# Two paddings in the allocation of SBUF: the start addresses of all matmul operands of an attention and two feed-forward layers

## The chip, the cores and the metric

The kernel runs on one core of a Trainium2 chip. The metric is device time in microseconds (us). The kernel before took 1613.8 us, the median of three runs (1612.5 to 1614.32).

## The reference

Two batches of 3008 tokens go through an attention without softmax and then, as 6016 tokens of 256 features, through two feed-forward layers with 2048 hidden features:

```
scores = (z @ z.T) / S                 # z: 2 x 3008 x 64
x = u * (max(scores, 0)**2 @ v)        # u, v: 2 x 3008 x 256
h = x @ w_in1;  g = where(h > 0, h, exp(min(h, 0)) - 1);  x = g @ w_out1
h = x @ w_in2
g = (a0 + a1 h + a2 h^2 + a3 h^3) / (1 + |b0| |h| + |b1| h^2 + 1e-6)
return g @ w_out2
```

The weights come as 64-bit floats and are brought to single precision on the chip.

## The kernel before, in words

Every product is computed in three matmuls on float32r operands: each float32 matrix is held as a rounded part (hi) and the rest (lo), and hi·hi, lo·hi and hi·lo are summed in PSUM. A matmul has a moving operand (`rhs`, here up to 512 columns, 4 bytes each, so 2048 bytes in each partition) and a stationary one (`lhsT`, 128 columns, 512 bytes), which a weight load brings into the array beforehand. The weight load of the next matmul runs while the present one streams.

The program has two stages. In the attention (about the first 520 us), queries are taken in spans of up to 512 columns (ten of 512 and two of 448), keys in chunks of 128. Here a matmul uses 64 of the 128 rows of the array, and two of them, on the two halves of the rows, run at the same time; the text calls them a pair. For each two chunks the PE does three pairs of scores (line 292) and then twelve pairs of values (line 329). Of one span of 512 columns that is 36 pairs of scores and 141 of values (the last chunk is a half). In the feed-forward part the tokens are taken in tiles of 512 columns (nine) and then 448, 384, 320 and 256. `hidden` (lines 263 to 265 in `mm3`, and 399, 400 and 402) and `project` use all 128 rows, 12 matmuls of a layer and of 128 hidden features. The order of all of this is written out by hand, step by step; VectorE, ScalarE and GpSimd work on other steps of it in the meantime.

Where a tile lies in SBUF follows from the order of the pools and their sizes, in each partition from address 0 on:

- a scratch of 16384 bytes for transfers that GpSimd would describe, reserved by the program object; then 128 bytes with four small constants;
- pool `wp`, 32 buffers of 4096 bytes (tag `w`): the split values V and all split weights. It starts at 16512, so all of its buffers and all of the 512-byte slices used as stationary operands start at 128 modulo 512. At the end of the program some tiles of the last feed-forward tile (256 columns) lie there too;
- pool `cp`, one tile `coef` of 6 floats (a and b of the last layer), which takes 32 bytes, at 147584;
- pool `sp`, everything else (tags `q`, `raw`, `rl`, `hl`, `x`, `x2`, `t`, `r`, `xo`, `e`), from 147616 on, in buffers of 2048 or 4096 bytes, so that all of them start at 160 modulo 512.

So the moving operand of a matmul starts at 160 modulo 512 in all 9240 matmuls but 96: those at the end take `w` tiles at 128. The stationary operand starts at 128 (V and weights), and at 160 in the 864 matmuls of the scores, whose two operands are both Z tiles (`rl`, `x2`, `t`, `r` of pool `sp`). A weight load in line 329 or in a feed-forward line reads at 128, one in line 292 at 160, and what streams beside it is the matmul before it in the program. No operand's start is 0 modulo 512.

## Time and profile before

| | |
|---|---|
| median of the three runs | 1613.8 us |
| span of the profiled execution | 1611.0 us |
| PE busy | 1569.5 us (97%), 9240 matmuls |
| VectorE (DVE) busy | 1392.3 us (86%) |
| ScalarE (ACT) busy | 1326.0 us (82%) |
| GpSimd (POOL) busy | 723.9 us (45%) |

The profile is of one execution, whose span (first to last instruction) is 2.8 us under the median of the runs. Matmuls are pipelined: the profile's duration of one (about 395 ns for 512 columns) is longer than the distance from its start to the next one's start, so busy time of PE says little, and the count of matmuls in a stretch says how fast they follow each other.

### The profile page before, as it was taken

To read this page: it belongs to the slowest core of one execution; us is meant where nothing else is said; L and a number is where in the kernel's file an instruction comes from. 1 tells how busy PE (TensorE), PEld (TensorE's weight loads), DVE (VectorE), ACT (ScalarE), POOL (GpSimd) and SP (SyncE) were. 2 spreads that over 40 slices of the span, in tenths; PEclk is the share of its full clock that TensorE was granted. 3 is DMA by queue.
4 is the path that set the end of the run, shared out by engine and by line. 5 is a ranking of instruction groups with operands and counts; after the bars stand their busy time and mean duration, and the time that the engine had idled before them with its cause. 6 is when DMAs were issued, how large, how long until landed. Compare 5 with 4: busy or idle time off the path is not lost.

```text
span 1611.0 us, 25201 instructions
## 1 busy us (share of the span) xinstructions
PE 1569.5 (97%) x9240; PEld 1321.5 (82%) x9240; DVE 1392.3 (86%) x1915; ACT 1326.0 (82%) x2123; POOL 723.9 (45%) x590
## 2 busy tenths in 40 slices
PE   8999999999999999999999999999999999999986
PEld 6888897898778778787878787887878888999976
DVE  7788889888886478989898988889898999999998
ACT  6777776877776788988888888988888888999886
POOL 3344542443433444445444444444454444444445
PEclk9999999999999999999999999999999999999999
DMA  4243343221222400000000000000000000000000
GB/s 125 66 125 119 112 144 109 66 68 50 75 61 89 157 26 1 27 1 1 27 1 27 1 27 1 27 0 1 25 1 23 1 22 1 20 1 12 11 1 15
DMA packets 38716, 67.16 MB, mean 42 GB/s; under 512 B 4928, under 2 KB 15680, under 8 KB 38592
## 3 DMA queue, kind: packets, MB, share of 16 engines
q1 hardware_dynamic: 38592, 65.55, 13.1%
q8 instruction: 72, 1.18, 0.3%
q14 instruction: 52, 0.43, 0.1%
HBM read 45.88 MB, written 19.66 MB: 41 GB/s over the span
## 4 chain that ended last, share of the span: by engine, by line
PE 66%; DVE 11%; issue 3%; ACT 3%; POOL 1%; POOLq 0%; ACTq 0%; DVEq 0%
PE psum L329 11%; PE psum L264 9%; PE psum L399 9%; PE psum L402 9%; PE psum L265 9%; PE psum L400 9%; PE psum L263 9%; PE psum L292 3%; DVE x L526 2%; DVE t L528 1%; DVE q L503 1%; DVE q L527 1%; DVE e L432 1%; DVE t L509 1%; ACT t L480 1%
## 5 line engine op out<-in xcount | busy, mean ns | idle before, releaser
L533 POOL TENSOR_TENSOR x<-t,r 128x512 fp32r<-128x512 f32 (+3 forms) x190 | 233.9, 1231 | 509.4 <-DVE t L528 443.3
L329 PE MATMUL psum<-hl,w 64*128 64x512 f32 (+1 forms) x2256 | 395.2, 391 | 3.7 <-ACT xo L349 2.6
L329 PEld LDWEIGHTS psum<-hl,w 64*128 64x128 f32 x2256 | 279.7, 185 | 44.4 <-ACT xo L349 6.4
L329 PE MATMUL psum<-x,w 64*128 64x512 f32 (+1 forms) x1128 | 293.1, 388 | 1.0 <-DVE x L305 1.0
L441 POOL TENSOR_TENSOR hl<-e,hl 128x512 fp32r<-128x512 f32 (+3 forms) x200 | 246.8, 1234 | 35.4 <-ACT hl L440 29.6
L295 ACT ACTIVATE w<-psum 128x1024 f32<-128x1024 f32 (+1 forms) x144 | 145.5, 1011 | 111.3 <-PE psum L292 109.8
L298 DVE SCALAR_TENSOR_TENSOR psum<-psum,w 128x1024 f32<-128x1024 f32 (+1 forms) x144 | 173.8, 1207 | 57.9 <-ACT w L295 57.2
L480 ACT ACTIVATE t<-psum,coef 128x512 f32<-128x512 f32 (+3 forms) x200 | 150.6, 753 | 78.8 <-PE psum L402 77.4
L503 DVE SCALAR_TENSOR_TENSOR q<-q,coef,psum 128x512 f32<-128x512 f32 (+3 forms) x190 | 135.3, 712 | 72.1 <-ACT q L496 71.5
L305 DVE TENSOR_TENSOR x<-psum,hl 128x1024 fp32r<-128x1024 f32 (+1 forms) x144 | 172.9, 1201 | 12.0 <-ACT q L200 0.5
L329 PEld LDWEIGHTS psum<-x,w 64*128 64x128 f32 x1128 | 168.0, 185 | 17.3 <-DVE x L305 1.5
L264 PE MATMUL psum<-hl,w 128*128 128x512 f32 (+4 forms) x416 | 157.2, 378 | 4.8 <-POOL hl L441 4.5
L399 PE MATMUL psum<-x,w 128*128 128x512 f32 (+4 forms) x416 | 155.6, 376 | 2.0 <-ACT x L451 1.4
L264 PE MATMUL psum<-x,w 128*128 128x512 f32 (+3 forms) x384 | 147.8, 385 | 8.5 <-POOL x L533 8.5
L263 PE MATMUL psum<-hl,w 128*128 128x512 f32 (+4 forms) x416 | 155.6, 374 | 0.2 <-ACT hl L440 0.2
L399 PE MATMUL psum<-rl,w 128*128 128x512 f32 (+4 forms) x416 | 155.5, 376 | 0.0
L265 PE MATMUL psum<-hl,w 128*128 128x512 f32 (+4 forms) x416 | 155.3, 373 | 0.0
L400 PE MATMUL psum<-x,w 128*128 128x512 f32 (+4 forms) x416 | 154.7, 374 | 0.0
L400 PE MATMUL psum<-rl,w 128*128 128x512 f32 (+4 forms) x416 | 154.4, 373 | 0.0
L296 ACT ACTIVATE hl<-w 128x1024 fp32r<-128x1024 f32 (+1 forms) x144 | 150.6, 1046 | 4.6
L432 DVE SCALAR_TENSOR_TENSOR e<-e,psum 128x512 f32<-128x512 f32 (+3 forms) x200 | 129.8, 649 | 27.8 <-ACT e L427 21.8
L526 DVE SCALAR_TENSOR_TENSOR x<-t,coef,r 128x512 fp32r<-128x512 f32 (+3 forms) x190 | 150.2, 791 | 0.0
(143 smaller groups left out, 3683.2 us busy)
## 6 DMA issues: line engine op xcount, KB each, us to landing
raw<-w_in_dram SPq DMA_DIRECT2D x16, 512.0 KB, 3.9
raw<-w_out_dram SPq DMA_DIRECT2D x16, 512.0 KB, 3.8
wd<-q SPq DMA_DIRECT2D x28, 256.0 KB, 2.3
raw<-wd SPq DMA_DIRECT2D x14, 512.0 KB, 3.4
raw<-v_dram SPq DMA_DIRECT2D x22, 256.0 KB, 2.9
raw<-uT_dram SPq DMA_DIRECT2D x10, 512.0 KB, 3.8
xd<-xo SPq DMA_DIRECT2D x20, 256.0 KB, 2.2
outT_dram<-xo SPq DMA_DIRECT2D x18, 256.0 KB, 2.2
```

The source lines that it names most:

```text
L263: nc.tensor.matmul(out, lhsT=lh, rhs=rh, start=start, stop=False)
L264: nc.tensor.matmul(out, lhsT=lh, rhs=rl, start=False, stop=False)
L265: nc.tensor.matmul(out, lhsT=ll, rhs=rh, start=False, stop=stop)
L298: nc.vector.scalar_tensor_tensor(out=s, in0=s, scalar=SCALE, in1=e, op0=ALU.mult, op1=ALU.mult)
L305: nc.vector.tensor_tensor(out=lo[:, :, :w], in0=psum[:, i:i + 2, :w], in1=f(hi[:, :, :w]), op=ALU.subtract)
L329: nc.tensor.matmul(acc[ti][d, h][:, :w], lhsT=lhs[rows, j % 2, d * P:(d + 1) * P], rhs=rhs[rows, :w], start=j == 0 and k == 0, stop=k == 2 ...
L399: nc.tensor.matmul(h[:, cols], lhsT=wh[:, d, c], rhs=x[d][0], start=d == 0, stop=False)
L400: nc.tensor.matmul(h[:, cols], lhsT=wl[:, d, c], rhs=x[d][0], start=False, stop=False)
L441: nc.gpsimd.tensor_tensor(out=lo, in0=e, in1=f(hi), op=ALU.subtract)
L480: act(new("p", "t", 3), h, AF.Identity, bias=a2, scale=a3)
L526: stt(out=st["hi"], in0=st["top"], scalar=a0, in1=st["r"], op0=ALU.add, op1=ALU.mult)
L533: eng.tensor_tensor(out=st["lo"], in0=st["p"], in1=st["r"], op=ALU.mult)
```

## The change

The pool `cp` is made first, before `wp`. Its tile `coef` gets 480 floats (1920 bytes), of which the first 6 are used; the others are a filler and are never written or read. The scratch is 8192 bytes instead of 16384. With that `coef` lies at 8320, `wp` starts at 10240 (20 times 512) and `sp` at 141312 (276 times 512). All buffers of both pools then start at 0 modulo 512, and so do both operands of all 9240 matmuls. Every operand of the other engines that lies in these pools moves along. No instruction is added, removed or moved on any engine, no wait changes, and each tile shares its buffer with the same other tiles as before.

```
-    wp = ctx.enter_context(tc.tile_pool(name="wp", bufs=32))
     cp = ctx.enter_context(tc.tile_pool(name="cp", bufs=1))
+    wp = ctx.enter_context(tc.tile_pool(name="wp", bufs=32))
     sp = ctx.enter_context(tc.tile_pool(name="sp", bufs=2))
...
-    coef = cp.tile([P, 6], F32, name="coef")
+    coef = cp.tile([P, 480], F32, name="coef")[:, :6]
...
-    nc = bacc.Bacc("TRN2", target_bir_lowering=False, num_devices=1)
+    nc = bacc.Bacc("TRN2", target_bir_lowering=False, num_devices=1, dynamic_dma_scratch_size=8192)
```

## Rows read from the trace of the kernel before

**Rows 1.** The page: busy time, slices of PE and its clock, chain that ended last
```profile
span 1611.0 us, 25201 instructions
PE 1569.5 (97%) x9240; PEld 1321.5 (82%) x9240; DVE 1392.3 (86%) x1915; ACT 1326.0 (82%) x2123; POOL 723.9 (45%) x590
...
PE   8999999999999999999999999999999999999986
...
PEclk9999999999999999999999999999999999999999
...
PE 66%; DVE 11%; issue 3%; ACT 3%; POOL 1%; POOLq 0%; ACTq 0%; DVEq 0%
```
**Rows 2.** Busy us (x instructions) by stretch; then clock, DMA share, GB/s
```profile
0.00:520.00 520.00, 504.94 (x4262) 432.43 (x4264) 435.99 (x447) 385.70 (x462) 211.01 (x171) 1.00 0.31 94
520.00:600.00 80.00, 76.65 (x321) 60.37 (x322) 42.73 (x68) 62.38 (x109) 36.25 (x28) 0.98 0.28 92
600.00:1250.00 650.00, 649.68 (x2778) 520.60 (x2777) 577.49 (x846) 566.06 (x955) 308.36 (x239) 1.00 0.04 12
1250.00:1500.00 250.00, 248.82 (x1261) 223.88 (x1260) 234.42 (x382) 227.12 (x429) 119.09 (x108) 1.00 0.03 9
1500.00:1611.00 111.00, 89.41 (x623) 84.18 (x623) 101.64 (x175) 84.74 (x170) 49.19 (x46) 0.98 0.03 10
```
**Rows 3.** Chain that ended last, 318 to 358: start us, us, what
```profile
322.60 0.69 PE psum L292 x6
323.28 2.79 PE psum L329 x24
...
346.96 0.69 PE psum L292 x6
```
**Rows 4.** Lines 292 and 329: matmuls, duration ns min/median/max, first and last start
```profile
L292 PE MATMUL psum<-rl,t x48: 385/387/393, 32.9 to 333.3; 64*128 64x512 f32 x48
L292 PE MATMUL psum<-rl,r x48: 385/387/393, 39.8 to 340.3; 64*128 64x512 f32 x48
L329 PE MATMUL psum<-hl,w x2256: 358/392/625, 9.0 to 520.2; 64*128 64x512 f32 x158, 64*128 64x448 f32 x30
...
L329 PE MATMUL psum<-x,w x1128: 357/391/625, 10.8 to 520.4; 64*128 64x512 f32 x158, 64*128 64x448 f32 x30
```
**Rows 5.** Matmul groups by shape: line, tiles, count, busy us, mean ns, idle before
```profile
L329 PE MATMUL psum<-hl,w 64*128 64x512 f32 x1880 | 337.3, 395 | 2.8 <-ACT xo L349 1.7 <-ACT hl L296 0.9
L329 PE MATMUL psum<-x,w 64*128 64x512 f32 x940 | 253.6, 392 | 1.0 <-DVE x L305 1.0
L263 PE MATMUL psum<-hl,w 128*128 128x512 f32 x288 | 114.2, 396 | 0.2 <-ACT hl L440 0.2
L265 PE MATMUL psum<-hl,w 128*128 128x512 f32 x288 | 113.8, 395 | 0.0
L265 PE MATMUL psum<-hl,w 128*128 128x448 f32 x32 | 11.8, 369 | 0.0
L265 PE MATMUL psum<-hl,w 128*128 128x384 f32 x32 | 10.9, 339 | 0.0
L265 PE MATMUL psum<-hl,w 128*128 128x320 f32 x32 | 9.9, 309 | 0.0
L265 PE MATMUL psum<-w 128*128 128x256 f32 x32 | 9.0, 282 | 0.0
L263 PE MATMUL psum<-w 128*128 128x256 f32 x32 | 9.0, 282 | 0.0
L263 PE MATMUL psum<-hl,w 128*128 128x256 f32 x32 | 9.0, 280 | 0.0
L265 PE MATMUL psum<-hl,w 128*128 128x256 f32 x32 | 8.9, 279 | 0.0
```
**Rows 6.** The page: large groups of ACT; DMA queue
```profile
L295 ACT ACTIVATE w<-psum 128x1024 f32<-128x1024 f32 (+1 forms) x144 | 145.5, 1011 | 111.3 <-PE psum L292 109.8
L296 ACT ACTIVATE hl<-w 128x1024 fp32r<-128x1024 f32 (+1 forms) x144 | 150.6, 1046 | 4.6
...
q1 hardware_dynamic: 38592, 65.55, 13.1%
```

## The prediction

> **What bounds the kernel now.** I read the page first. PE is busy in 97% of the span, every slice but the first and the last two shows it at 9, and the chain of work that ended last is PE for 66% [rows 1]. Busy time of matmuls is modelled, so I went on to the table by stretches for their number. From 600 to 1250 us, where only tiles of 512 columns run, PE has 649.68 of 650 us and 2778 matmuls [rows 2]: 650 / 2778 = 234.0 ns from one start to the next, without a gap worth naming. DVE is at 577.5 / 650 = 89% there and ACT at 87%, close behind but hidden. In the attention (0 to 520 us) PE has 505 of 520, and a step of three pairs of scores and twelve of values takes, over seven steps in the chain from 322.60 to 346.96, 24.36 / 7 / 15 = 232.0 ns a pair [rows 3]. Only after 1500 us is PE idle for long (89 of 111 us). So up to 1500 us the time is the number of matmuls by their distance, and an edit that moves no instruction can matter by that distance alone.

> [...]

> **The change part by part.** First the small parts. The shorter scratch serves transfers described by GpSimd; all transfers here are on the hardware queue [rows 6], so it costs nothing, and nothing comes up in its place. The filler is never touched, and the six coefficients are read as before. ACT, DVE and POOL operands move by 32 or 160 bytes. The nearest rows are two ACT instructions of equal size: L295 writes tiles at 128 modulo 512 (1011 ns), L296 reads those and writes at 160 (1046 ns) [rows 6]. They also differ in their source, PSUM or SBUF, so 35 ns, 3.5%, is the most that I grant to addresses, in either direction. ACT and DVE have 11 to 13% to spare beside PE in the long stretch, which covers it; without that cover 3.5% of DVE's 577 us there would be 20 us. I take 0.

> What is left is the distance between matmuls, and the kernel before holds an experiment on it. Score matmuls (line 292) have their moving and their stationary operand in the same pool, both at 160 modulo 512. For the others the weights lie at 128 while 160 streams. Now the durations: in line 292 the median is 387 ns and the longest 393, in two groups of 48 [rows 4]. These two numbers belong to places in the six. The first four matmuls, during which another Z tile is loaded, take 386 to 387; the last two, during which a V tile at 128 is loaded, 392 to 393. Line 329, where nearly always a V tile is next, has a median of 392 [rows 4]. The streamed tile is at 160 in all of these, so what differs is the tile that is loaded beside it. Duration and distance go together (392 with 232, 395 with 234, both 160 or 161 more), so 387 is a distance of about 227. The price of the unequal start is thus 5 ns (392 against 387) to 6 ns (393 against 387), and 7 ns from 234 to 227.

> [...]

> After the change both operands start at 0, so they are at equal addresses modulo 512, as in the scores. I take 6 ns for each matmul or pair that loads unequally now:
> - feed-forward, 512 columns: 12 groups of 288 like the two shown [rows 5], 3456 matmuls x 6 ns = 20.7 us;
> - attention, 512 columns: 1880 + 940 values matmuls are 1410 pairs [rows 5]. The last of each step loads a Z tile, but the third pair of scores loads a V tile, so the number stays 1410: x 6 ns = 8.5 us. The scores themselves gain nothing more;
> - narrower tiles: durations of 369, 339, 309 and 279 for 448, 384, 320 and 256 columns [rows 5]. [...] At 256 columns the kernel before has equal starts too, with `w` tiles at 128 on both sides: 282 against 279 or 280 [rows 5], no gain but 2 to 3 ns of loss. I take 0 for all of them; by 2 ns lost on 4992 - 3456 = 1536 matmuls it would be 3 us, by 3 ns gained -5 us.

> Sum: 29 us less. The 11 to 13% that DVE and ACT have to spare are more than the 2.6% taken from PE, so little of it comes back as waits; I give back 2 us for the last stretch, where PE waits for others anyway. 1611.0 - 27 = 1584 us of span, and with the 2.8 us by which the median of the runs lies above the span, 1587 us. The case's own range: 5 ns and 20% given back, 4866 x 5 x 0.8 = 19 us, gives 1595; 7 ns and 3 us from narrow tiles gives 34 + 3, 1577.

> **The rivals.**
> [...]

> *No change.* The scores are quicker not because the starts agree but because of what Z tiles are: in the pool of the streamed tiles, and few. Both stay as they are, and values and weights stay at 234. Or only the stationary start counts, 160 is good, and 0 is like 128. Against the first: the last two matmuls of the six stream Z tiles too and are slow. The second I can't exclude. 1614.

> *Slower: the two reads meet.* With equal starts the stream and the weight load begin at the same place modulo 512 within a few ns, and one holds up the other. For it: the 256-wide rows, 282 against 279 or 280, the only ones with aligned starts on both sides of the `w` pool. Against it: the scores. 2.5 ns on 4992 feed-forward matmuls and 2124 pairs (3384 values and 864 score matmuls of the 9240, halved, and the rest) [rows 1, 4] is 18 us: 1632. It decides if a matmul that starts at 0 is held up by more than the 6 ns that the equal start gives.

> **How the numbers follow.** Equal starts as in the scores, 1587 us: 0.49. The excess goes wholly or for the most part (below 1575): 0.19. No change: 0.18. Slower: 0.14. A difference under 0.2% (3 us) can't be told from none here. Faster is then 0.68, same 0.17 and slower 0.15. For 8 in 10 the range takes in the first and the third case, the greater part of the second (to 1522) and the smaller mishaps of the last (to 1622); the likeliest case's own range is 1577 to 1595.

> **What would show it.** If I am right, the stretch 600 to 1250 holds about 2850 matmuls in place of 2778, a feed-forward matmul of 512 columns lasts 389 ns in place of 395, line 329 goes from 392 to 387, the 393 disappears from line 292, and the durations of ACT and DVE stay. [...] If line 292 gets longer than 387, reads meet. If 329 and the feed-forward lines keep 392 and 395, the start is not what made the scores quick. I am wrong in the step that matters most if (0, 0) does not act as (160, 160).

## The result, and the profile after

The changed kernel takes 1585.2 us (median of four runs, 1583.6 to 1586.8), the kernel before 1613.2 us beside it: a ratio of 0.983, 95% interval 0.981 to 0.984. 28 us are gone, and 1587 us was forecast. The profiled execution has a span of 1584.6 us. The page shows the same instructions, and busy times of DVE, ACT and POOL that differ by under 0.2% [rows 1]; only PE's own has fallen, by 30 us. (One execution of e5, an experiment below, took 8726 us against 1610 to 1613 of its nine others, and no reading rests on it.)

```profile
span 1584.6 us, 25201 instructions
...
PE 1539.4 (97%) x9240; PEld 1312.4 (83%) x9240; DVE 1390.4 (88%) x1915; ACT 1325.3 (84%) x2123; POOL 723.2 (46%) x590
...
PE 65%; DVE 10%; ACT 4%; issue 4%; POOL 2%; POOLq 0%; ACTq 0%; DVEq 0%
```

Where it went is seen in a table by stage, cut so that each stretch holds the same number of matmuls in both kernels: attention, feed-forward up to the last tile's `w` operands, and the rest. The columns are the stretch, its length, PE's busy time (x matmuls), clock, DMA share and GB/s. First the kernel before:

```profile
0.00:520.20 520.20, 505.14 (x4264) 1.00 0.31 94
520.20:1583.10 1062.90, 1047.02 (x4849) 1.00 0.05 17
1583.10:1611.00 27.90, 17.33 (x133) 0.96 0.03 10
```

and the changed one:

```profile
0.00:514.80 514.80, 499.24 (x4264) 1.00 0.30 95
514.80:1555.60 1040.80, 1022.73 (x4849) 1.00 0.05 17
1555.60:1584.60 29.00, 17.45 (x133) 0.97 0.06 21
```

So 5.4 us come from the attention, 22.1 us from the feed-forward part, and the end is 1.1 us longer.

Something that is not the change's shifts the first two of these. In the changed kernel's execution the granted clock stood at 0.50 from 98 to 101 us, and PE got 16 matmuls through where the kernel before, at 1.00, had 26. In the kernel before such a fall lies near 588 us, in the feed-forward part, where the changed one has none (same columns; first before, then changed):

```profile
98.00:101.00 3.00, 3.00 (x26) 1.00 0.03 5
587.00:592.00 5.00, 5.00 (x15) 0.66 0.23 85
```
```profile
98.00:101.00 3.00, 3.00 (x16) 0.50 0.18 72
587.00:592.00 5.00, 5.00 (x23) 1.00 0.01 3
```

The step of the attention in which it falls (from one first start of line 292 to the next) takes 6.88 us in the changed kernel and 5.26 us before, so it costs about 1.6 us. With the clock alike in both, an estimate from these numbers is 7 us for the attention and 20.5 us for the feed-forward part; the sum of the two stays.

In the stretch that answers to the third of [rows 2], 2847 matmuls stand in place of 2778, that is 228.3 ns from start to start in place of 234.0; DVE is at 592.5 / 650 = 91% there:

```profile
600.00:1250.00 650.00, 647.23 (x2847) 533.59 (x2846) 592.53 (x867) 578.27 (x977) 315.66 (x245) 1.00 0.03 12
```

By line (matmuls, duration min/median/max, first and last start), line 292 has lost its 393 and line 329 its 392 [rows 4]:

```profile
L292 PE MATMUL psum<-rl,t x48: 386/386/387, 33.1 to 330.8; 64*128 64x512 f32 x48
...
L329 PE MATMUL psum<-hl,w x2256: 355/386/794, 9.1 to 514.8; 64*128 64x512 f32 x158, 64*128 64x448 f32 x30
```

By shape (count, busy us, mean ns, idle before), 512 columns went from 395 or 396 to 389 or 390 and 448 from 369 to 364 in the groups shown (the twelve groups of 448 columns lost 1 to 5 ns each, 2.6 in the mean), 320 stayed at 309, and 256 columns got longer, 279 to 283 [rows 5]:

```profile
L263 PE MATMUL psum<-hl,w 128*128 128x512 f32 x288 | 112.4, 390 | 0.3 <-ACT hl L440 0.3
...
L265 PE MATMUL psum<-hl,w 128*128 128x512 f32 x288 | 112.2, 389 | 0.0
...
L265 PE MATMUL psum<-hl,w 128*128 128x448 f32 x32 | 11.6, 364 | 0.0
...
L265 PE MATMUL psum<-hl,w 128*128 128x320 f32 x32 | 9.9, 309 | 0.0
...
L265 PE MATMUL psum<-hl,w 128*128 128x256 f32 x32 | 9.1, 283 | 0.0
```

The chain in the attention (start, us, what) has steps of 3.40 us in place of 3.48 [rows 3]; the twelve pairs of values went from 2.79 to 2.72:

```profile
320.36 0.68 PE psum L292 x6
321.04 2.72 PE psum L329 x24
323.75 0.68 PE psum L292 x6
...
333.95 0.68 PE psum L292 x6
```

### The profile page after: what moved, and what is told of

It reads as the page before. It is cut to its first block, busy times and chain, and to the rows that moved or that the text cites. A ratio compares the mean times of both kernels' runs of the same rounds, so it can differ in the third digit from the quotient of the medians.

```text
span 1584.6 us, 25201 instructions
## 1 busy us (share of the span) xinstructions
PE 1539.4 (97%) x9240; PEld 1312.4 (83%) x9240; DVE 1390.4 (88%) x1915; ACT 1325.3 (84%) x2123; POOL 723.2 (46%) x590
## 4 chain that ended last, share of the span: by engine, by line
PE 65%; DVE 10%; ACT 4%; issue 4%; POOL 2%; POOLq 0%; ACTq 0%; DVEq 0%
PE psum L329 11%; PE psum L264 9%; PE psum L399 9%; PE psum L402 9%; PE psum L400 9%; PE psum L265 9%; PE psum L263 8%; PE psum L292 3%; DVE x L526 1%; DVE t L528 1%; DVE q L503 1%; DVE q L527 1%; POOL hl L441 1%; DVE t L509 1%; DVE e L432 1%
## 5 line engine op out<-in xcount | busy, mean ns | idle before, releaser
L329 PE MATMUL psum<-hl,w 64*128 64x512 f32 (+1 forms) x2256 | 383.1, 388 | 4.2 <-ACT xo L349 3.1
L329 PEld LDWEIGHTS psum<-hl,w 64*128 64x128 f32 x2256 | 265.5, 186 | 45.4 <-ACT xo L349 7.5
L329 PE MATMUL psum<-x,w 64*128 64x512 f32 (+1 forms) x1128 | 275.9, 385 | 0.4 <-DVE x L305 0.4
L295 ACT ACTIVATE w<-psum 128x1024 f32<-128x1024 f32 (+1 forms) x144 | 145.7, 1012 | 105.8 <-PE psum L292 104.3
L329 PEld LDWEIGHTS psum<-x,w 64*128 64x128 f32 x1128 | 156.1, 186 | 16.2 <-DVE x L305 1.1
L264 PE MATMUL psum<-hl,w 128*128 128x512 f32 (+4 forms) x416 | 155.5, 374 | 8.0 <-POOL hl L441 7.9
L399 PE MATMUL psum<-x,w 128*128 128x512 f32 (+4 forms) x416 | 153.1, 370 | 2.1 <-ACT x L451 1.4
L296 ACT ACTIVATE hl<-w 128x1024 fp32r<-128x1024 f32 (+1 forms) x144 | 150.3, 1044 | 4.6
L263 PE MATMUL psum<-hl,w 128*128 128x512 f32 (+4 forms) x416 | 153.7, 369 | 0.3 <-ACT hl L440 0.3
L265 PE MATMUL psum<-hl,w 128*128 128x512 f32 (+4 forms) x416 | 153.4, 369 | 0.0
L399 PE MATMUL psum<-rl,w 128*128 128x512 f32 (+4 forms) x416 | 152.9, 370 | 0.0
L400 PE MATMUL psum<-x,w 128*128 128x512 f32 (+4 forms) x416 | 152.9, 370 | 0.0
L400 PE MATMUL psum<-rl,w 128*128 128x512 f32 (+4 forms) x416 | 152.6, 369 | 0.0
```

The costliest lines, as they stand in the source:

```text
L263: nc.tensor.matmul(out, lhsT=lh, rhs=rh, start=start, stop=False)
L264: nc.tensor.matmul(out, lhsT=lh, rhs=rl, start=False, stop=False)
L265: nc.tensor.matmul(out, lhsT=ll, rhs=rh, start=False, stop=stop)
L329: nc.tensor.matmul(acc[ti][d, h][:, :w], lhsT=lhs[rows, j % 2, d * P:(d + 1) * P], rhs=rhs[rows, :w], start=j == 0 and k == 0, stop=k == 2 ...
L399: nc.tensor.matmul(h[:, cols], lhsT=wh[:, d, c], rhs=x[d][0], start=d == 0, stop=False)
L400: nc.tensor.matmul(h[:, cols], lhsT=wl[:, d, c], rhs=x[d][0], start=False, stop=False)
```

## The experiments

All move tiles by a filler in `coef` or by an untouched tile between the pools, except the half loads and the one with the order alone. "Distance" is the start of the moving operand less that of the stationary one, modulo 512; the scores, both of whose operands lie in `sp`, have distance 0 in every kernel. Times are medians, and each ratio is to runs of the kernel before made beside that kernel; 1614.1 us is their median in the last round (25 runs). "Spacing" is 650 us over the number of matmuls between 600 and 1250 us, waits included.

In that stretch the granted clock is 1.00 in every profile. Near the end of the program it is not alike: it stood at 0.5 for 7 to 10 us on end in e2, e4 and e9 to e12 (below, e2: stretch, length, PE's busy time, clock, DMA share, GB/s), and for no more than 4 us in the kernel before. So the spacing is the surer column, and slow kernels whose totals lie within 3 us of each other are not ranked by them.

```profile
1598.00:1608.50 10.50, 7.52 (x36) 0.52 0.00 0
```

| run | stationary, moving (modulo 512) | distance | us | ratio to before (95%) | spacing ns |
|---|---|---|---|---|---|
| before | 128, 160 | 32 | 1614.1 | | 234.0 |
| changed | 0, 0 | 0 | 1585.2 | 0.983 (0.981 to 0.984) | 228.3 |
| e1 | 160, 160 | 0 | 1586.1 | 0.983 (0.982 to 0.984) | 228.3 |
| e8, order alone | 160, 160 | 0 | 1585.4 | 0.982 (0.981 to 0.983) | 228.2 |
| e3 | 0, 256 | 256 | 1587.6 | 0.983 (0.982 to 0.985) | 228.2 |
| e4 | 0, 64 | 64 | 1595.2 | 0.989 (0.987 to 0.990) | 230.3 |
| e2 | 0, 32 | 32 | 1613.8 | 1.000 (0.999 to 1.001) | 234.0 |
| e6 | 32, 0 | -32 | 1612.9 | 0.999 (0.998 to 1.000) | 234.0 |
| e11 | 0, 96 | 96 | 1614.0 | 1.000 (0.999 to 1.001) | 234.0 |
| e5, e9 | 0, 128 | 128 | 1611.6 | 0.998 (0.997 to 0.999) | 233.2 |
| e10 | 0, 192 | 192 | 1612.6 | 0.999 (0.998 to 1.000) | 234.0 |
| e12 | 0, 288 | 288 | 1612.8 | 1.000 (0.999 to 1.001) | 234.0 |
| e7, half loads | 0, 0 | 0 | 1591.5 | 0.985 (0.984 to 0.987) | 230.5 |

**Equal starts at no round address** (e1_both_160).

```
-    coef = cp.tile([P, 480], F32, name="coef")[:, :6]
+    coef = cp.tile([P, 520], F32, name="coef")[:, :6]
```

> Both pools start at 160 modulo 512, so both operands of all matmuls do: equal, but at no round address. If equal starts are what counts: as the changed kernel, 1585 us, feed-forward matmuls of 512 columns last 389 ns and follow each other after 227 ns. If a start at 0 modulo 512 (or at 64 or 128) is what counts: 1613 us, 395 ns, 234 ns as before.

1586.1 us: the whole gain, with both operands at 160 modulo 512. The stretch and the lines are those of the changed kernel:

```profile
600.00:1250.00 650.00, 647.24 (x2847) 533.43 (x2846) 592.40 (x868) 578.17 (x976) 314.33 (x244) 1.00 0.04 12
```
```profile
L329 PE MATMUL psum<-hl,w x2256: 355/386/792, 8.9 to 513.8; 64*128 64x512 f32 x158, 64*128 64x448 f32 x30
```

So 0 modulo 512 is not what makes it quicker, nor a boundary of 64 or 128.

**The old distance with the weights at 0** (e2_streamed_32).

```
-    sp = ctx.enter_context(tc.tile_pool(name="sp", bufs=2))
+    gap = ctx.enter_context(tc.tile_pool(name="gap", bufs=1)); sp = ctx.enter_context(tc.tile_pool(name="sp", bufs=2))
...
-    coef = cp.tile([P, 480], F32, name="coef")[:, :6]
+    coef = cp.tile([P, 480], F32, name="coef")[:, :6]; gap.tile([P, 8], F32, name="between")
```

> Stationary operands at 0 modulo 512, moving ones at 32: the same distance of 32 bytes as before, shifted so that the weights lie at 0. Equal starts count: 1613 us, 395 ns, score matmuls still 386 to 387 for the first four of six. A stationary operand at 0 is enough: 1585 us. A moving operand on an odd multiple of 32 is what hurts: 1613 us too, but then the scores, both at 32, get slow as well (393).

1613.8 us, no change from before. Line 329 is back at 391, and line 292 has its 393 again, while its first matmuls keep 386 although they stream from 32:

```profile
L292 PE MATMUL psum<-rl,t x48: 386/386/393, 33.3 to 333.9; 64*128 64x512 f32 x48
...
L329 PE MATMUL psum<-hl,w x2256: 358/391/792, 9.1 to 520.7; 64*128 64x512 f32 x158, 64*128 64x448 f32 x30
```

A stationary operand at 0 is not enough (1613.8 us), and a streamed operand at an odd multiple of 32 does no harm by itself (386 ns here, streamed from 32; 1586.1 us in e1, streamed from 160). With e1 this leaves the distance.

**Distances of 256 and 64** (e3_streamed_256, e4_streamed_64: the filler between the pools has 64 and 16 floats).

> Stationary operands at 0, moving ones at 256 modulo 512. If the starts have to be equal modulo 512: 234 ns a matmul and 1613 us. If modulo 64, 128 or 256 is enough, or both only have to lie on a boundary of 64: 227 ns and 1585 us. [...]

> Stationary operands at 0, moving ones at 64 modulo 512. Equal modulo 64 is enough: 227 ns, 1585 us. Equal modulo more than 64: slower than that, 231 to 240 ns, 1605 to 1640 us.

256 is as good as 0 (1587.6 us, a spacing of 228.2 ns), so the period is not 512, and being apart brings nothing on top. 64 gives two thirds of the gain (1595.2 us). Its matmuls are mixed: the means of the twelve feed-forward groups of 512 columns run from 389 to 399 (two of them in the second fence), 448 columns take 360 to 366 ns where the changed kernel has 364 to 370, and the scores, whose operands are equal here too, are now slow in most of their six (medians by place 394, 394, 386, 386, 393, 393). The pairs of values follow each other after 226, 229 and 232 ns in turn (medians by place in the step), though the starts of all of them are 64 apart:

```profile
L292 PE MATMUL psum<-rl,t x48: 385/393/394, 31.2 to 330.0; 64*128 64x512 f32 x48
```
```profile
L263 PE MATMUL psum<-x,w 128*128 128x512 f32 x288 | 113.0, 392 | 0.0
...
L265 PE MATMUL psum<-hl,w 128*128 128x512 f32 x288 | 112.4, 390 | 0.0
...
L265 PE MATMUL psum<-hl,w 128*128 128x448 f32 x32 | 11.5, 360 | 0.0
```

**A distance of 128** (e5_streamed_128, e9_streamed_128_again: 32 floats).

> Stationary operands at 0, moving ones at 128 modulo 512. With 256 the matmuls followed each other after 227 ns (1587 us), with 64 after 226 to 232 (1595 us). Equal modulo 128 is enough: all at 226 to 227, 1586 us. Equal modulo 256 is needed: as with 64 or worse, 229 to 234 ns, 1595 to 1614 us.

> The kernel with streamed operands at 128 once more, for its profile, since the profiled execution of the first one was disturbed. Its time was 1611.6 us; so 512-wide feed-forward matmuls should follow each other after 233 to 234 ns, and score matmuls, whose operands are both at 128, should last 386.

1611.6 us: equal modulo 128 is not enough. The profile is that of e9. The spacing is 233.2, but the scores, expected at 386, last 392 in the median:

```profile
L292 PE MATMUL psum<-rl,t x48: 383/392/396, 33.2 to 334.0; 64*128 64x512 f32 x48
...
L329 PE MATMUL psum<-hl,w x2256: 355/389/792, 8.7 to 520.8; 64*128 64x512 f32 x158, 64*128 64x448 f32 x30
```

**The other sign** (e6_weights_32: `coef` with 488 floats, the tile between with 120).

> Stationary operands at 32, moving ones at 0: the distance of before with the other sign. If only the difference of the starts counts and its sign does not: 1613 us, 234 ns. If the moving operand's own start counted (0 here, 160 before, 32 in the run with 1614 us): 1585 us.

1612.9 us and 234 ns. The streamed operands lie at 0 here, as in the changed kernel, and nothing is won.

**Three more distances** (e10_streamed_192, e11_streamed_96, e12_streamed_288: 48, 24 and 72 floats between the pools).

> Stationary operands at 0, moving ones at 192. Distances so far: 0 and 256: 1585 to 1588 us; 64: 1595; 32, 128 and minus 32: 1612 to 1614. If the time repeats with 256 and is the same on both sides of 0: as 64 (192 = 256 - 64), 1595 us. If only multiples of 256 are good and 64 is a lucky case: 1605 to 1615 us.

> Stationary operands at 0, moving ones at 96. If time grows with the distance from the nearest multiple of 256 up to 128: between 64 and 128, 1600 to 1610 us. If an odd multiple of 32 is bad in itself: 1612 to 1616 us. If some distance lets the two reads miss each other: below 1585 us.

> Stationary operands at 0, moving ones at 288 = 256 + 32. If the time repeats with 256, as with 32: 1613 us, 234 ns. If a distance of 256 is good because it is large: about 1587 us.

288 behaves as 32 (1612.8 and 1613.8 us), as 256 behaves as 0 (1587.6 and 1585.2): over those two pairs the time repeats with 256. It is not symmetric, since 192 is slow (1612.6) where 64 is half good (1595.2), and it does not grow with the distance, since 96 is as slow as 32 (1614.0 and 1613.8). At 512 columns no distance tried is quicker than 0 by more than 0.1 ns of spacing.

**Half loads** (e7_half_load): what a load of half the columns does to the matmul that streams beside it.

```
-        nc.tensor.matmul(out, lhsT=lh, rhs=rl, start=False, stop=False)
-        nc.tensor.matmul(out, lhsT=ll, rhs=rh, start=False, stop=stop)
+        nc.tensor.matmul(out[:64], lhsT=lh[:, :64], rhs=rl, start=False, stop=False)
+        m = P if stop else 64; nc.tensor.matmul(out[:m], lhsT=ll[:, :m], rhs=rh, start=False, stop=stop)
...
-                nc.tensor.matmul(h[:, cols], lhsT=wl[:, d, c], rhs=x[d][0], start=False, stop=False)
+                nc.tensor.matmul(h[:64, cols], lhsT=wl[:, d, half], rhs=x[d][0], start=False, stop=False)
...
+            nc.tensor.matmul(h[:64, cols], lhsT=wh[:, 0, half], rhs=x[0][1], start=False, stop=False)
+            nc.tensor.matmul(h[:, cols], lhsT=wh[:, 1, c], rhs=x[1][1], start=False, stop=True)
```

> The changed kernel, but 7 of the 12 feed-forward matmuls of each group of hidden features and layer (both corrections of the project step except at its end, three of four in the hidden step) load 64 columns instead of 128, and so leave out half of these corrections; the number of streamed columns stays. [...]

A load of 64 columns does last less itself, 135 ns against 188 for 128 columns. But with such loads beside the stream the kernel is slower than the changed one, 1591.5 against 1585.2 us, at a spacing of 230.5 ns against 228.3:

```profile
L264 PE MATMUL psum<-x,w 128*64 128x512 f32 x288 | 113.2, 393 | 0.0
...
L399 PE MATMUL psum<-x,w 128*128 128x512 f32 x288 | 112.0, 389 | 0.0
...
L401 PE MATMUL psum<-x,w 128*64 128x512 f32 x144 | 55.8, 388 | 0.0
```

The three lines stream the same number of columns, with all starts at 0, and last 393, 389 and 388. The load that comes next, and so runs beside them, is of 64 columns for the first two and of 128 for the third. So a load of fewer columns does not shorten the matmul beside it, and equal starts are not the whole condition: in this kernel, whose loads are of unequal length, the group of line 264 lasts 393 ns where the changed one has 390.

**The order alone** (e8_order_alone): the kernel before with this edit and no other.

```
+    cp = ctx.enter_context(tc.tile_pool(name="cp", bufs=1))
     wp = ctx.enter_context(tc.tile_pool(name="wp", bufs=32))
-    cp = ctx.enter_context(tc.tile_pool(name="cp", bufs=1))
```

> The kernel before with its coefficient pool made first and nothing else: no filler, the scratch of 16384 bytes. Both pools of matmul operands then start at 160 modulo 512. Equal starts count: 1585 us, 227 ns, the whole gain without filler and smaller scratch. The scratch or the round address has a part in it: between 1590 and 1613 us.

1585.4 us. The 32 bytes of `coef` now lie ahead of both pools instead of between them, both start at 160, and the whole gain is there:

```profile
600.00:1250.00 650.00, 647.24 (x2848) 533.53 (x2847) 592.39 (x868) 578.72 (x977) 314.84 (x245) 1.00 0.04 12
```

Filler and smaller scratch add nothing to it. None of the runs beats the changed kernel by more than the spread of the times.

## Why the prediction was right, point by point

**What bounds.** PE's pace did. The distance between matmuls fell by 5.7 ns in the long stretch, waits included, and the span followed, 26.4 us in the profiled executions against 27 forecast. (The prediction's "89 of 111 us" after 1500 us is PE's busy time; idle it is for 22 of them [rows 2].)

**The price, 6 ns.** It came out for 512 columns as a change of duration: 395 to 389, 392 to 386. From start to start it is nearer to the 7 ns that the prediction had also read: in the feed-forward part the median went from 234 to 227, and in the attention 80 ns a step over its twelve unequal pairs are 6.7. That the cost belongs to the distance of the two starts and not to an address is shown by e1 and e8 (equal at 160: quick) against e2 and e6 (32 apart, one of them at 0: slow). That the start that counts is that of the tile loaded beside the stream, and not that of the matmul's own, is seen in the kernel before: the last pair of scores, whose own tile is at 160 while one at 128 is loaded, takes 392 to 393 ns, and the last pair of values of a step, whose own is at 128 while one at 160 is loaded, 386 to 387 (medians by place in the step). e1 and e2 differ in no instruction and by 28 us (1586.1 and 1613.8), at a spacing of 228.3 and 234.0 ns: the pace of the stream depends here on where the tile that is loaded beside it lies, seen from the streamed one.

**The sum.** Feed-forward at 512 columns: 20.7 us forecast; the stretch of all widths gave 22.1, about 20.5 with the clock alike. Narrow tiles were put at 0; 448 columns gained 2.6 ns in the mean (about 1 us on 384 matmuls) and 256 columns lost 3 to 4 ns, which the 256-wide rows with both operands in `w` had shown [rows 5]. Attention: 8.5 us forecast, 5.4 found, about 7 with the clock alike. The pace itself gave more than forecast there: 3.48 - 3.40 = 0.08 us a step, 9.4 us over the 1410 pairs of values or some 118 steps of 512 columns. Some 4 us of it did not arrive: 1.6 us by the clock, and part of the rest as longer waits of weight loads (total us, times, longest; before 9.3 and 6.4):

```profile
PEld psum L292 <- DVE x L305: 10.4, 13, 2.0
...
PEld psum L329 <- ACT xo L349: 7.5, 11, 1.5
```

In the feed-forward part a new wait stands at the end of each 512-wide tile from 635 us on, where line 264 meets POOL's split of `hl` before it is done (start, us, what, idle before): PE reaches it earlier now. Over the program this wait of PE went from 4.5 to 7.9 us, and in the feed-forward stretch of the table by stage PE's time without a matmul from 15.9 to 18.1 us.

```profile
635.72 0.62 ACT L440 CAST hl<-e 128x512 fp32r<-128x512 f32 x1 [1.48 <-DVE e L432]
...
635.82 0.50 PE L264 MATMUL psum<-hl,w 128*128 128x512 f32 x1 [0.36 <-POOL hl L441]
```

So the 2 us that were given back were too few for the waits, and 6 ns was a little too small a price. These two errors have opposite signs and nearly cancel: the mechanism of the forecast is borne out, but that it came within 2 us is in part luck.

**Small parts.** ACT's and DVE's totals did not move with their addresses: in the thirteen profiles of the table, quick and slow, DVE is busy for 1389.5 to 1392.4 us and ACT for 1325.2 to 1326.3. And e8 shows that scratch and filler cost and bring nothing.

**The rivals.** No change and slower are out with the time. The weight load does begin 3 ns after the matmul beside it (median in the kernel before, 600 to 1250 us), but with equal starts that matmul got shorter, not longer. The case below 1575 us is out too: no run shows how short the distance of two matmuls of 512 columns can get, and no distance tried has a spacing under 228 ns (227 from start to start without waits). The prediction's reading of the scores was right in its result and too simple in its terms. Equal modulo 512 is more than is needed (256 will do). And "what is loaded beside it" does not settle a single matmul at every distance: the scores have equal starts in all kernels, and last 386 or 387 at distances 0, 32, 256 and 288 of the other matmuls, but 390 to 393 in the median at 64, -32, 96, 128 and 192. So something else must count as well; that it is what went before them is a guess, which no run tries by itself. Why unequal starts cost anything, and why 64 is half good, stays open.

## What to carry to other kernels

Where a kernel is bound by back-to-back matmuls, compare the durations and the spacing of matmuls of equal shape with each other; if they differ while no wait shows (387 and 393 ns in line 292 here), look at the addresses of the operands. In this kernel the starts that agree modulo 256 bytes were the quick ones (distances 0 and 256: 1585.2 and 1587.6 us, all others 1595.2 to 1614.1), so try streamed tiles and weights that do. One small tile between their pools, the 32 bytes of `coef`, was enough to spoil it, and making it first was enough to mend it (e8, 1585.4 us). That is worth 6 to 7 ns of a matmul of 512 columns, 1 to 5 at 448 and nothing at 320, and it costs 3 to 4 at 256, so here it is the wide matmuls that one counts. A group in the same kernel that happens to have the other layout, as the scores here, prices such an edit ahead of time.
